# Operands of a second layer's output products: made for two pairs at a time, products in another order, VectorE's share in a written order

## The chip, the cores and the metric

One core of a Trainium2 chip. The time is the device time of one execution in microseconds. The engines are named as the profile names them: PE (TensorE's matmuls), PEld (its weight loads), DVE (VectorE), ACT (ScalarE), POOL (GpSimd), SP (SyncE, which issues most of the DMA transfers).

## The reference

A chunked attention is followed by two feed-forward layers, in float32. The part around the change is the second layer:

```python
def _moe2_ref(x, w_in, w_out, alpha):      # x 3072 x 512, w_in 512 x 2048, w_out 2048 x 512
    h = x @ w_in
    g = np.maximum(h, 0.0) + alpha * np.minimum(h, 0.0)
    return (g @ w_out).astype(np.float32)
```

## The kernel before

The first layer and the attention take the first 580 us or so and are not touched. The second layer works on three blocks of 1024 tokens (`NB`), each in an h stage (x times w_in, with the PReLU) and then a y stage (g times w_out). Both matrix products are done by a scheme of seven half-size products for eight (Strassen-like), so that a block's y stage has seven products, numbered 1 to 7, and each sums over eight pairs of 128-row feature tiles (`P2` is 8). A matmul here multiplies 128x128 by 128x512. To keep float32 accuracy each operand is split in a high half (the value rounded to FP32R, by ACT) and a low half (value minus high half, by DVE or POOL), and three matmuls take (high, high), (high, low), (low, high); one pair of one product is 2 output tiles x 3 = 6 matmuls.

The h stage: `pair_h(i)` (line 422) makes, for one pair, the products 1, 6, 5, 7, 2, 3, 4 of h (`product`, line 408), adds banks together on DVE (line 425), copies on ACT (lines 443 and 450), and applies the PReLU (`prelu`: ACT lines 416 and 417, then DVE line 418). The results lie in two tiles of the pool `w`: gx holds the g of tokens and features that the code calls ga[0] and gb[1], gy holds ga[1] and gb[0]. POOL then forms two differences, d3 = gb[1] - ga[1] (line 459, tile t3) and ga[1] = ga[1] - ga[0] (line 460).

The y stage: `prep(b, s)` (line 471) makes the operand of step s, that is of one product and one pair: ACT copies the high half (line 481) and DVE or POOL subtracts the low half (line 483; POOL has product 1's pairs 2 to 7, and every fourth pair of products 5, 2, 7, 3 and 4). Product 6 needs a sum first (line 478, into a PSUM bank `yb`) and leaves a difference for product 4 (line 485). `y_product` (line 491) issues the 6 matmuls of a step (line 502), `y_done` (line 508) combines banks and writes the output. `ORDER` is the order of the products, 1, 6, 5, 2, 7, 3, 4. Operands are asked for `LEAD` steps ahead, and the first `EARLY` of them before the last pair of the h stage.

The loads: `load_out` (line 359) brings the weights of two steps (512 KB, four buffers, freed by the matmuls), `load_in` (line 365) those of a pair of h, `load_x2` (line 375) the next block's x; line 384 forms sums of x and line 132 (POOL) with line 131 (ACT) splits them for the next h stage. All of these loads go through SP's queue.

The order of instructions on each engine is not the order of the code: a scheduler places them by its own estimates, within the dependences and within `tc.issue_after(...)`, which puts what is written under it behind a named instruction. The pool `w` has 34 buffers of 4 KB a partition, shared by g, the operands, x and half of the weights.

Of the kernel before, what the change touches and what calls it, by code (L numbers as in the profile page):

```python
# [7 lines left out]
FP32 = mybir.dt.float32  # L8
# [26 lines left out]
def chunk_attention_two_ffn_kernel(  # L35
# [12 lines left out]
    nc = tc.nc  # L48
# [14 lines left out]
    def f32(ap):  # L63
        return ap.bitcast(FP32)
# [289 lines left out]
    gx = {}  # L354
    gy = {}
    t3 = {}
# [8 lines left out]
    def load_in(i, q):  # L365
        p = i % P2
        n = 2 if q < 3 else 1
        pool, tag = (w_p, "w") if i % 2 == 0 else (stage["z"], "z")
        w = pool.tile([128, 2, n, 256], FP32R, tag=tag, name="wi2")
        nc.sync.dma_start(  # L370
            out=f32(w).rearrange("p a s n -> p (a s n)"),
            in_=w2i[p][:, 1024 * q:1024 * q + 512 * n])
        win[i, q] = w
# [47 lines left out]

    def pair_h(i):
        b, p = divmod(i, P2)
        f = 2 * p
        add = lambda o, p, q: nc.vector.tensor_tensor(out=o, in0=p, in1=q, op=ALU.add)
        d = {}
        x = gx[b, p] = w_p.tile([128, 2, 512], FP32, tag="w", name="gx")
        y = gy[b, p] = w_p.tile([128, 2, 512], FP32, tag="w", name="gy")
        if p % 2 == 0:
            t3[b, p // 2] = zr.tile([128, 2, 512], FP32, tag="t3", name="t3")  # L430
        d3 = t3[b, p // 2][:, p % 2]
        ga, gb = (x[:, 0], y[:, 0]), (y[:, 1], x[:, 1])

# [37 lines left out]
    def prep(b, s):  # L471
        mi, p = divmod(s, P2)
        m = ORDER[mi]
        x, y, d3 = gx[b, p], gy[b, p], t3[b, p // 2][:, p % 2]
        op = w_p.tile([128, 2, 512], FP32R, tag="w", name="go")
        if m == 6:
            src = y_bank(b, 7)
            nc.vector.tensor_tensor(out=src, in0=d3, in1=x[:, 0], op=ALU.add)  # L478
        else:
            src = {1: x[:, 0], 5: y[:, 0], 2: y[:, 1], 7: d3, 3: x[:, 1], 4: x[:, 0]}[m]  # L480
# [10 lines left out]
    def y_product(b, s, tiles=(0, 1)):  # L491
        mi, p = divmod(s, P2)
        m = ORDER[mi]
        into = {2: 1, 3: 5, 4: 7}.get(m, m)
        if m == into and p == 0 and 0 in tiles:
            yd[b, m] = [y_bank(b, m) for _ in range(2)]
        w = wo2[b * NO + mi * (P2 // 2) + p // 2][:, p % 2]
        w = w.rearrange("k a (i n) -> k a i n", i=2)
        op = gop[b, s]
        for i in tiles:  # L500
            for n, (a, c) in enumerate(PASS):
                nc.tensor.matmul(  # L502
                    out=yd[b, into][i], lhsT=w[:, a, i], rhs=op[:, c],
                    start=(m == into and p == 0 and n == 0), stop=(p == P2 - 1 and n == 2),
                    skip_group_check=True,
                )

    def y_done(b, m, tiles=(0, 1)):
        add = lambda o, p, q: nc.vector.tensor_tensor(out=o, in0=p, in1=q, op=ALU.add)
        if m in (1, 6, 5):  # L510
            for i in tiles:
                tag = "gl" if m == 6 else "gh"
                e = ye[b, m, i] = g_p.tile([128, 512], FP32, tag=tag, name="ye")
                d = yd[b, m][i]
                if m == 6:
                    add(e, d, ye[b, 1, i])
# [235 lines left out]
    if True:  # L752
# [192 lines left out]
        for b in range(NB):  # L945
            more = b + 1 < NB
            for p in range(P2):
                i = b * P2 + p
                if p == P2 - 1:
                    for s in range(EARLY):  # L950
                        prep(b, s)
                if i > 0:
                    pair_h(i)
                for q in range(4):
# [5 lines left out]
            if more:  # L960
# [88 lines left out]
```

## Time and profile before

| | |
|---|---|
| median of 3 runs | 1084.25 us (1084.19 to 1084.38) |
| profiled execution, its own time | 1085.27 us |
| its span, first to last instruction | 1083.5 us |
| PE busy | 1049.8 us, 97% of the span |
| DVE, ACT, POOL busy | 681.0, 545.9, 470.9 us |
| second layer on PE | from 580.1 to 1078.4 us |

The page gives the share of busy time over the whole span; a stage is read from the stretches, the chain and the timeline. Since matmuls overlap, a busy PE may still have lost time, which shows in the number of matmuls that a stretch holds.

### The profile page before, as it was taken

How to read it: one execution, taken by the hardware profiler on the slowest of the kernel's cores; microseconds unless marked ns; L12 is line 12 of the kernel's file. 1: busy time of each engine (PE TensorE's matmuls, PEld its weight loads, DVE VectorE, ACT ScalarE, POOL GpSimd, SP SyncE). 2: the span in 40 equal slices, each digit the busy share in tenths (PEclk: the TensorE clock that was granted, in tenths of full speed). 3: DMA queues.
4: the chain of work that ended last, by engine and by line, in shares of the span. 5: the costliest groups of instructions: out<-in, count | busy, mean ns of one | idle time of the engine just before them, and what ended most of it. 6: DMA issues, size and time to landing. Idle time of an engine off the chain costs nothing.

```text
span 1083.5 us, 17665 instructions
## 1 busy us (share of the span) xinstructions
PE 1049.8 (97%) x6624; PEld 855.5 (79%) x6624; DVE 681.0 (63%) x1085; ACT 545.9 (50%) x986; POOL 470.9 (43%) x355
## 2 busy tenths in 40 slices
PE   4989999999999999999999999999999899999998
PEld 3767788888888888888888888778888688888786
DVE  6869855855755585576311355799456898456873
ACT  5657744544544454354342365555356654466650
POOL 3656744534545453354372122538123466123430
PEclk9989999999999999999999999999999999999999
DMA  9744254644654464454520463578844678733476
GB/s 318 285 162 155 89 174 128 233 138 167 212 190 170 138 220 136 181 199 145 177 68 1 168 221 137 178 247 274 248 160 163 192 248 275 230 139 144 156 211 167
DMA packets 99364, 196.19 MB, mean 181 GB/s; under 512 B 36560, under 2 KB 50896, under 8 KB 99280
## 3 DMA queue, kind: packets, MB, share of 16 engines
q1 hardware_dynamic: 93712, 188.52, 52.3%
q10 hardware_dynamic: 5568, 6.56, 1.8%
q8 instruction: 52, 0.85, 0.3%
q14 instruction: 32, 0.26, 0.1%
HBM read 153.10 MB, written 41.94 MB: 180 GB/s over the span
## 4 chain that ended last, share of the span: by engine, by line
PE 84%; DVE 6%; ACT 4%; issue 3%; POOL 2%; DMA 1%; SPq 0%; DVEq 0%; POOLq 0%; ACTq 0%
PE h L273 23%; PE y L313 22%; PE h L408 20%; PE yb L502 16%; PE pv L684 2%; PE sp L589 2%; DVE yb L478 1%; DVE go L483 1%; ACT go L481 1%; POOL wt L132 1%; DVE gx L485 1%; ACT wt L131 0%; ACT u L108 0%; ACT eb L666 0%; ACT n L416 0%
## 5 line engine op out<-in xcount | busy, mean ns | idle before, releaser
L273 PE MATMUL h<-ring,wt 128*128 128x512 f32 x1152 | 285.7, 395 | 7.1 <-ACT wt L131 4.1
L273 PEld LDWEIGHTS h<-ring,wt 128*128 128x128 f32 x1152 | 217.9, 190 | 56.2 <-ACT wt L131 4.8
L502 PE MATMUL yb<-go,wo 128*128 128x512 f32 x1008 | 235.4, 391 | 6.4 <-DVE go L483 2.7
L502 PEld LDWEIGHTS yb<-go,wo 128*128 128x128 f32 x1008 | 187.8, 188 | 51.7 <-DVE go L483 5.4
L408 PE MATMUL h<-xh,wi 128*128 128x512 f32 x672 | 211.9, 391 | 0.7 <-DVE gx L418 0.4
L295 POOL TENSOR_TENSOR gl<-t,gh 128x512 fp32r<-128x512 f32 x96 | 127.3, 1328 | 154.9 <-ACT gh L294 126.3
L313 PE MATMUL y<-gh,wt 128*128 128x512 f32 x768 | 193.4, 391 | 0.0
L313 PEld LDWEIGHTS y<-gh,wt 128*128 128x128 f32 x768 | 143.1, 188 | 30.5
L287 DVE TENSOR_TENSOR t<-h,t 128x512 f32<-128x512 f32 x96 | 66.0, 687 | 139.9 <-ACT t L286 139.9
L408 PEld LDWEIGHTS h<-xh,wi 128*128 128x128 f32 x672 | 126.1, 188 | 30.7 <-ACT hv L450 2.9
L286 ACT ACTIVATE t<-h 128x512 f32<-128x512 f32 x96 | 56.9, 593 | 113.4 <-PE h L273 98.9
L459 POOL TENSOR_TENSOR t<-gx,gy 128x512 f32<-128x512 f32 x24 | 31.1, 1296 | 175.7 <-DVE gy L418 175.7
L313 PE MATMUL y<-gl,wt 128*128 128x512 f32 x384 | 104.3, 389 | 0.0
L294 ACT ACTIVATE gh<-t 128x512 fp32r<-128x512 f32 x96 | 60.3, 628 | 47.9 <-DVE t L287 44.1
L313 PEld LDWEIGHTS y<-gl,wt 128*128 128x128 f32 x384 | 72.1, 188 | 15.0
L408 PE MATMUL h<-xl,wi 128*128 128x512 f32 x192 | 74.7, 389 | 0.0
L132 POOL TENSOR_TENSOR ws<-sm,ws 128x512 fp32r<-128x512 f32 x32 | 42.5, 1328 | 63.9 <-ACT ws L131 47.6
L417 ACT ACTIVATE n<-n,alpha_neg 128x512 f32<-128x512 f32 x96 | 65.9, 719 | 0.6
L483 DVE TENSOR_TENSOR go<-gx,go 128x512 fp32r<-128x512 f32 x42 | 57.3, 1404 | 1.4 <-ACT go L481 1.4
L132 POOL TENSOR_TENSOR wt<-s,wt 128x512 fp32r<-128x512 f32 x32 | 41.3, 1292 | 37.4 <-ACT wt L131 37.0
L408 PE MATMUL h<-x,wi 128*128 128x512 f32 x144 | 56.1, 389 | 0.0
L115 DVE TENSOR_SCALAR u<-u 128x512 uint32<-128x512 uint32 x64 | 44.2, 695 | 14.3 <-ACT u L108 14.2
(92 smaller groups left out, 1348.0 us busy)
## 6 DMA issues: line engine op xcount, KB each, us to landing
wo<-w2o SPq DMA_DIRECT2D x84, 512.0 KB, 4.1
wi<-w2i SPq DMA_DIRECT2D x72, 512.0 KB, 5.0
kn<-in_k_dram SPq DMA_DIRECT2D x24, 384.0 KB, 4.3
vn<-in_v_dram SPq DMA_DIRECT2D x24, 384.0 KB, 3.9
ri<-in_moe_w_in_dram SPq DMA_DIRECT2D x16, 512.0 KB, 9.9
ro<-in_moe_w_out_dram SPq DMA_DIRECT2D x16, 512.0 KB, 9.8
pk<-in_moe_w_in_dram SPq DMA_DIRECT2D x16, 512.0 KB, 4.1
pk<-in_moe_w_out_dram SPq DMA_DIRECT2D x16, 512.0 KB, 4.2
```

The source lines that it names most:

```text
L115: nc.vector.tensor_scalar(out=u, in0=u, scalar1=3, scalar2=None, op0=ALU.logical_shift_left)
L132: nc.gpsimd.tensor_tensor(out=lo, in0=v, in1=f32(hi), op=ALU.subtract)
L273: last["ffn"] = nc.tensor.matmul(out=h, lhsT=wi[:, a, kk, :], rhs=ring[c][:, s0:s0 + n, kk, :], start=(i == 0), stop=(i == 3 * KD - 1),).ins
L286: nc.scalar.activation(out=t, in_=h, func=ACTF.Tanh)
L287: last["dve"] = nc.vector.tensor_tensor(out=t, in0=h, in1=t, op=ALU.subtract).ins
L294: nc.scalar.activation(out=gh, in_=t, func=ACTF.Copy)
L295: nc.gpsimd.tensor_tensor(out=gl, in0=t, in1=f32(gh), op=ALU.subtract)
L313: mm = nc.tensor.matmul(out=yp[l, b][j][:, :n * 128], lhsT=wo[:, a, j * 128:(j + 1) * 128], rhs=g[c], start=first, stop=final,)
L408: nc.tensor.matmul(out=h, lhsT=w[:, a, 128 * kt:128 * kt + 128], rhs=x[c][:, kt, :], start=(first and j == 0), stop=(j == 5), skip_group_c ...
L417: nc.scalar.activation(out=n, in_=n, func=ACTF.Copy, scale=alpha_neg[:, f:f + 1])
L483: eng.tensor_tensor(out=op[:, 1], in0=src, in1=f32(op[:, 0]), op=ALU.subtract)
L502: nc.tensor.matmul(out=yd[b, into][i], lhsT=w[:, a, i], rhs=op[:, c], start=(m == into and p == 0 and n == 0), stop=(p == P2 - 1 and n == ...
```

## The change

`prep` now makes the operand of two pairs at once: its ACT copy and its DVE subtraction are 128x1024 where they were 128x512, in two tiles (goh, gol) where one tile (go) held both halves of one pair. For that the four g of two pairs lie beside each other in four tiles (ga0, ga1, gb0, gb1; `gq` in place of gx and gy). All subtractions are DVE's; POOL has none of them. The order of the products is 1, 5, 2, 6, 7, 3, 4. Product 6's sum is made in place in ga0 and product 4's difference in place in gb0, both in SBUF. The first half of product 1's operands is asked for before the last pair of h, the second half within it (`ahead`), before that pair's last PReLU; DVE's part of every `prep` is chained (`last["prep"]`). The loads of `load_in` are chained too, and the next block's x is asked for one product earlier (s >= P2, it was 2 * P2). `y_done` copies or adds the banks of 5 only after product 6.

```diff
-    ORDER = (1, 6, 5, 2, 7, 3, 4)
+    ORDER = (1, 5, 2, 6, 7, 3, 4)
-    LEAD = 6
-    EARLY = 4
+    LEAD = 4
+    EARLY = 2
...
-        nc.sync.dma_start(
+        with tc.issue_after(last["load"]):
+            last["load"] = nc.sync.dma_start(
...
-    def pair_h(i):
+    def pair_h(i, ahead=None):
...
-        x = gx[b, p] = w_p.tile([128, 2, 512], FP32, tag="w", name="gx")
-        y = gy[b, p] = w_p.tile([128, 2, 512], FP32, tag="w", name="gy")
         if p % 2 == 0:
+            for n in ("ga0", "ga1", "gb0", "gb1"):
+                gq[b, n, p // 2] = w_p.tile([128, 2, 512], FP32, tag="w", name=n)
...
         product(d[7], i, 4, False)
-        prelu(gb[0], d[7], f + 1)
+        if ahead is None:
+            prelu(gb[0], d[7], f + 1)
+        else:
+            with tc.issue_after(last["pre"]):
+                ahead()
+            with tc.issue_after(last["prep"]):
+                prelu(gb[0], d[7], f + 1)
...
     def prep(b, s):
-        mi, p = divmod(s, P2)
+        mi, pp = divmod(s, P2 // 2)
...
+        def dve(out, p, q, op):
+            with tc.issue_after(last["prep"]):
+                last["prep"] = nc.vector.tensor_tensor(out=out, in0=p, in1=q, op=op).ins
+
         if m == 6:
-            src = y_bank(b, 7)
-            nc.vector.tensor_tensor(out=src, in0=d3, in1=x[:, 0], op=ALU.add)
...
-        nc.scalar.activation(out=op[:, 0], in_=src, func=ACTF.Copy)
-        eng = nc.gpsimd if (m == 1 and p > 1) or (m not in (1, 6) and p % 4 == 3) else nc.vector
-        eng.tensor_tensor(out=op[:, 1], in0=src, in1=f32(op[:, 0]), op=ALU.subtract)
-        if m == 6:
-            nc.vector.tensor_tensor(out=x[:, 0], in0=y[:, 1], in1=src, op=ALU.subtract)
-        gop[b, s] = op
+            dve(ga0, d3, ga0, ALU.add)
+        if m == 4:
+            dve(gb0, gb0, ga0, ALU.subtract)
+        src = {1: ga0, 6: ga0, 5: ga1, 2: gb0, 7: d3, 3: gb1, 4: gb0}[m]
+        hi = w_p.tile([128, 2, 512], FP32R, tag="w", name="goh")
+        lo = w_p.tile([128, 2, 512], FP32R, tag="w", name="gol")
+        nc.scalar.activation(out=hi, in_=src, func=ACTF.Copy)
+        dve(lo, src, f32(hi), ALU.subtract)
+        gop[b, s] = hi, lo
...
-                if s >= 2 * P2 and s % 2 == 0 and early:
+                if s >= P2 and s % 2 == 0 and early:
```

What this does to the order of the instructions is shown at three places.

DVE in block 0, from the last pair's PReLUs (line 418) on, before (line 483 makes low halves, line 478 product 6's sums, line 485 product 4's differences):

```order
L418 SCALAR_TENSOR_TENSOR gx<-gx,n 128x512
L418 SCALAR_TENSOR_TENSOR gx<-h_6915,n 128x512
L418 SCALAR_TENSOR_TENSOR gy<-h_6917,n 128x512
L418 SCALAR_TENSOR_TENSOR gy<-h_6918,n 128x512
L478 TENSOR_TENSOR yb<-t_6295,gx 128x512 x2
L483 TENSOR_TENSOR go<-yb,go 128x512
L485 TENSOR_TENSOR gx<-gy,yb 128x512
L483 TENSOR_TENSOR go<-yb,go 128x512
L485 TENSOR_TENSOR gx<-gy,yb 128x512
L478 TENSOR_TENSOR yb<-t_6493,gx 128x512 x2
L483 TENSOR_TENSOR go<-yb,go 128x512
```

The same place now (line 484 makes all of a prep's DVE part; gol is the low half):

```order
L418 SCALAR_TENSOR_TENSOR ga_6825<-h_6911,n 128x512
L418 SCALAR_TENSOR_TENSOR ga_6826<-h_6913,n 128x512
L484 TENSOR_TENSOR gol<-ga_6658,goh 128x1024
L484 TENSOR_TENSOR gol<-ga_6825,goh 128x1024
L418 SCALAR_TENSOR_TENSOR gb_6827<-h_6914,n 128x512
L484 TENSOR_TENSOR gol<-ga_6294,goh 128x1024
L484 TENSOR_TENSOR gol<-ga_6492,goh 128x1024
L484 TENSOR_TENSOR gol<-ga_6659,goh 128x1024
L484 TENSOR_TENSOR gol<-ga_6826,goh 128x1024
L484 TENSOR_TENSOR gol<-gb_6295,goh 128x1024
```

Product 6's sums and differences no longer follow the PReLUs; the rest of product 1's low halves comes ahead of the last PReLU, and products 5 and 2 follow.

PE in block 0, pair 3 of h, before (h_6580 is the bank of product 7 and h_6579 that of 5, into which product 3 is added; h_6662 belongs to pair 4):

```order
L408 MATMUL h_6580<-xh,wi_6487 128x512
L408 MATMUL h_6580<-xl,wi_6487 128x512
L408 MATMUL h_6580<-xh,wi_6487 128x512 x2
L408 MATMUL h_6580<-xl,wi_6487 128x512
L408 MATMUL h_6580<-xh,wi_6487 128x512
L408 MATMUL h_6579<-xh,wi_6487 128x512
L408 MATMUL h_6579<-x_5828,wi_6487 128x512
L408 MATMUL h_6579<-xh,wi_6487 128x512 x2
L408 MATMUL h_6579<-x_5828,wi_6487 128x512
L408 MATMUL h_6579<-xh,wi_6487 128x512
L408 MATMUL h_6662<-xh,wi_6567 128x512
```

The same rows now (h_6664 belongs to pair 4):

```order
L408 MATMUL h_6580<-xh,wi_6487 128x512
L408 MATMUL h_6580<-xl,wi_6487 128x512
L408 MATMUL h_6580<-xh,wi_6487 128x512 x2
L408 MATMUL h_6580<-xl,wi_6487 128x512
L408 MATMUL h_6580<-xh,wi_6487 128x512
L408 MATMUL h_6664<-xh,wi_6569 128x512
L408 MATMUL h_6664<-x_5794,wi_6569 128x512
L408 MATMUL h_6664<-xh,wi_6569 128x512 x2
L408 MATMUL h_6664<-x_5794,wi_6569 128x512
L408 MATMUL h_6664<-xh,wi_6569 128x512
L408 MATMUL h_6579<-xh,wi_6487 128x512
```

Product 1 of the next pair now stands between products 7 and 3; before, product 3 came right behind product 7. The same swap is made in pair 5, and in both pairs of the other two blocks.

SP's queue in block 0 around the loads of the next block's x, before (w2o names the weights of the y stage, with the number of two pairs; y1d holds x):

```order
L362 DMA wo<-w2o_3_112 128x1024
L362 DMA wo<-w2o_0_105 128x1024
L362 DMA wo<-w2o_1_106 128x1024
L362 DMA wo<-w2o_2_107 128x1024
L378 DMA x_7201<-y1d 128x1024
L378 DMA x_7223<-y1d 128x1024
L378 DMA x_7245<-y1d 128x1024
L378 DMA x_7267<-y1d 128x1024
L362 DMA wo<-w2o_3_108 128x1024
L362 DMA wo<-w2o_0_93 128x1024
```

The same loads now:

```order
L361 DMA wo<-w2o_1_106 128x1024
L361 DMA wo<-w2o_2_107 128x1024
L361 DMA wo<-w2o_3_108 128x1024
L378 DMA x_7082<-y1d 128x1024
L361 DMA wo<-w2o_0_93 128x1024
L378 DMA x_7102<-y1d 128x1024
L378 DMA x_7122<-y1d 128x1024
L361 DMA wo<-w2o_1_94 128x1024
L378 DMA x_7142<-y1d 128x1024
L361 DMA wo<-w2o_2_95 128x1024
```

Before, the four x loads stand in one run behind eleven weight tiles of the y stage; now they stand behind eight to ten and are spread among them.

## Rows read from the trace of the kernel before

**Rows 1.** The page, part 1: busy time, share of the span, instructions.
```profile
PE 1049.8 (97%) x6624; PEld 855.5 (79%) x6624; DVE 681.0 (63%) x1085; ACT 545.9 (50%) x986; POOL 470.9 (43%) x355
```

**Rows 2.** The chain that ended last, block 0: start us, us, what.
```profile
614.50 27.21 PE h L408 x120
...
641.74 0.71 DVE h L425
...
642.47 0.61 ACT hv L450
```

**Rows 3.** Stretch: us, busy (count) of PE, PEld, DVE, ACT, POOL, PEclk, DMA.
```profile
614.50:1078.50 464.00, 456.90 (x1986) 369.96 (x1985) 316.97 (x413) 250.24 (x433) 177.69 (x110) 1.00 0.61 198
```

**Rows 4.** Line 502: duration ns min/median/max, first and last start us.
```profile
L502 PE MATMUL yb<-go,wo x1008: 387/389/504, 680.4 to 1078.4; 128*128 128x512 f32 x168
```

**Rows 5.** Four more stretches, columns as in rows 3.
```profile
690.50:719.50 29.00, 26.97 (x113) 20.38 (x112) 28.10 (x38) 17.32 (x32) 13.02 (x10) 1.00 0.73 252
719.50:779.50 60.00, 60.00 (x266) 49.65 (x265) 45.34 (x47) 25.58 (x40) 29.65 (x15) 1.00 0.80 249
846.00:872.00 26.00, 22.79 (x96) 17.24 (x95) 23.89 (x30) 16.14 (x30) 13.48 (x10) 1.00 0.71 239
1005.00:1024.00 19.00, 17.87 (x75) 13.21 (x74) 17.23 (x26) 9.67 (x18) 7.51 (x7) 1.00 0.51 166
```

**Rows 6.** Groups of DVE, 690.5 to 719.5 us.
```profile
L478 DVE TENSOR_TENSOR yb<-t,gx 128x512 f32<-128x512 f32 x8 | 6.6, 864 | 0.0
L483 DVE TENSOR_TENSOR go<-yb,go 128x512 fp32r<-128x512 f32 x8 | 5.5, 684 | 0.2
L485 DVE TENSOR_TENSOR gx<-gy,yb 128x512 f32<-128x512 f32 x8 | 5.4, 675 | 0.0
```

**Rows 7.** Timeline of PE, h stage: start us, us, engine, line, op, shapes, count.
```profile
641.99 0.62 PE L408 MATMUL h<-xh,wi 128*128 128x512 f32 x2
642.67 0.95 PE L408 MATMUL h<-xh,wi 128*128 128x512 f32 x2
...
944.47 0.50 PE L408 MATMUL h<-xh,wi 128*128 128x512 f32 x1 [0.36 <-DVE gx L418]
```

**Rows 8.** Lines 384, 131, 460: duration ns min/median/max.
```profile
L384 DVE TENSOR_TENSOR xt<-x,x x6: 1212/1216/1225, 528.9 to 881.3; 128x1024 f32<-128x1024 f32 x6
...
L131 ACT ACTIVATE xh<-xt x8: 1037/1048/1052, 731.6 to 903.9; 128x1024 fp32r<-128x1024 f32 x8
...
L460 POOL TENSOR_TENSOR gy<-gy,gx x24: 1286/1296/1732, 620.9 to 1011.0; 128x512 f32<-128x512 f32 x24
```

**Rows 9.** Timeline of the last pair of h, block 0, PE and DVE.
```profile
686.47 0.69 DVE L418 SCALAR_TENSOR_TENSOR gx<-h,n 128x512 f32<-128x512 f32 x1
...
689.02 2.88 PE L502 MATMUL yb<-go,wo 128*128 128x512 f32 x12
...
692.29 9.36 PE L502 MATMUL yb<-go,wo 128*128 128x512 f32 x40 [0.39 <-POOL go L483]
```

**Rows 10.** Lines 483 and 132, DVE and POOL: duration ns min/median/max.
```profile
L483 DVE TENSOR_TENSOR go<-gx,go x42: 641/1182/2896, 679.0 to 1068.6; 128x512 fp32r<-128x512 f32 x42
...
L483 POOL TENSOR_TENSOR go<-t,go x6: 1284/1769/7426, 719.1 to 1042.2; 128x512 fp32r<-128x512 f32 x6
...
L132 POOL TENSOR_TENSOR xl<-xt,xh x8: 2396/2846/2862, 735.3 to 909.2; 128x1024 fp32r<-128x1024 f32 x8
```

**Rows 11.** Timeline of SP and PE around the x loads of block 1.
```profile
705.67 2.29 SPq L378 DMA_DIRECT2D x<-y1d  x4
709.46 8.07 SPq L362 DMA_DIRECT2D wo<-w2o  x4
...
718.08 1.17 PE L502 MATMUL yb<-go,wo 128*128 128x512 f32 x4 [0.89 <-ACT go L481]
```

**Rows 12.** Time from issue to landing: x issued 704:708, then wo issued 708:711.
```profile
DMA to landing us min/median/max: 5.4/8.5/9.1
...
DMA to landing us min/median/max: 8.5/8.5/8.5
```

More of the change, by code (lines that the diff above doesn't have):

```diff
@@ L353, in chunk_attention_two_ffn_kernel @@
     xin = {}
-    gx = {}
-    gy = {}
+    gq = {}
     t3 = {}
@@ L369, in load_in @@
         w = pool.tile([128, 2, n, 256], FP32R, tag=tag, name="wi2")
-        nc.sync.dma_start(
-            out=f32(w).rearrange("p a s n -> p (a s n)"),
-            in_=w2i[p][:, 1024 * q:1024 * q + 512 * n])
+        with tc.issue_after(last["load"]):
+            last["load"] = nc.sync.dma_start(
+                out=f32(w).rearrange("p a s n -> p (a s n)"),
+                in_=w2i[p][:, 1024 * q:1024 * q + 512 * n]).ins
         win[i, q] = w
@@ L426, in pair_h @@
         d = {}
-        x = gx[b, p] = w_p.tile([128, 2, 512], FP32, tag="w", name="gx")
-        y = gy[b, p] = w_p.tile([128, 2, 512], FP32, tag="w", name="gy")
         if p % 2 == 0:
+            for n in ("ga0", "ga1", "gb0", "gb1"):
+                gq[b, n, p // 2] = w_p.tile([128, 2, 512], FP32, tag="w", name=n)
             t3[b, p // 2] = zr.tile([128, 2, 512], FP32, tag="t3", name="t3")
         d3 = t3[b, p // 2][:, p % 2]
-        ga, gb = (x[:, 0], y[:, 0]), (y[:, 1], x[:, 1])
+        ga, gb = [[gq[b, f"g{r}{k}", p // 2][:, p % 2] for k in range(2)] for r in "ab"]
         for m in (1, 6, 5, 7) if p % 2 else (6, 1, 5, 7):
@@ L471, in prep @@
     def prep(b, s):
-        mi, p = divmod(s, P2)
+        mi, pp = divmod(s, P2 // 2)
         m = ORDER[mi]
-        x, y, d3 = gx[b, p], gy[b, p], t3[b, p // 2][:, p % 2]
-        op = w_p.tile([128, 2, 512], FP32R, tag="w", name="go")
-        if m == 6:
-            src = y_bank(b, 7)
-            nc.vector.tensor_tensor(out=src, in0=d3, in1=x[:, 0], op=ALU.add)
-        else:
-            src = {1: x[:, 0], 5: y[:, 0], 2: y[:, 1], 7: d3, 3: x[:, 1], 4: x[:, 0]}[m]
-        nc.scalar.activation(out=op[:, 0], in_=src, func=ACTF.Copy)
-        eng = nc.gpsimd if (m == 1 and p > 1) or (m not in (1, 6) and p % 4 == 3) else nc.vector
-        eng.tensor_tensor(out=op[:, 1], in0=src, in1=f32(op[:, 0]), op=ALU.subtract)
-        if m == 6:
-            nc.vector.tensor_tensor(out=x[:, 0], in0=y[:, 1], in1=src, op=ALU.subtract)
-        gop[b, s] = op
+        ga0, ga1, gb0, gb1 = [gq[b, n, pp] for n in ("ga0", "ga1", "gb0", "gb1")]
+        d3 = t3[b, pp]
+        def dve(out, p, q, op):
+            with tc.issue_after(last["prep"]):
+                last["prep"] = nc.vector.tensor_tensor(out=out, in0=p, in1=q, op=op).ins
+        if m == 6:
+            dve(ga0, d3, ga0, ALU.add)
[7 more added lines that the diff above has]
+        gop[b, s] = hi, lo
     yd = {}
@@ L502, in y_product @@
                 nc.tensor.matmul(
-                    out=yd[b, into][i], lhsT=w[:, a, i], rhs=op[:, c],
+                    out=yd[b, into][i], lhsT=w[:, a, i], rhs=op[c][:, p % 2],
                     start=(m == into and p == 0 and n == 0), stop=(p == P2 - 1 and n == 2),
@@ L509, in y_done @@
         add = lambda o, p, q: nc.vector.tensor_tensor(out=o, in0=p, in1=q, op=ALU.add)
-        if m in (1, 6, 5):
+        if m == 5:
+            return
+        if m in (1, 6):
             for i in tiles:
[L512 to L516, printed above, removed]
+                e = ye[b, m, i] = g_p.tile([128, 512], FP32, tag="gl" if m == 6 else "gh", name="ye")
+                if m == 1:
+                    nc.scalar.activation(out=e, in_=yd[b, 1][i], func=ACTF.Copy)
                     continue
-                if m == 5:
-                    add(d, d, ye[b, 6, i])
+                add(e, yd[b, 6][i], ye[b, 1, i])
+                d = yd[b, 5][i]
+                add(d, d, e)
+                e = ye[b, 5, i] = g_p.tile([128, 512], FP32, tag="gh", name="ye")
                 nc.scalar.activation(out=e, in_=d, func=ACTF.Copy)
@@ L949, in chunk_attention_two_ffn_kernel, with ahead @@
                 if p == P2 - 1:
+                    last["prep"] = last["pre"]
                     for s in range(EARLY):
                         prep(b, s)
+                def ahead():
+                    for s in range(EARLY, P2 // 2):
+                        prep(b, s)
                 if i > 0:
-                    pair_h(i)
+                    pair_h(i, ahead if p == P2 - 1 else None)
                 for q in range(4):
@@ L964, in chunk_attention_two_ffn_kernel @@
                 late += [lambda q=q: load_in((b + 1) * P2 + 1, q) for q in range(4)]
-            with tc.issue_after(last["pre"]):
-                for s in range(EARLY, LEAD):
-                    prep(b, s)
             for s in range(7 * P2):
-                if s + LEAD < 7 * P2:
+                if s % 2 == 0 and s // 2 + LEAD < NO:
                     with tc.issue_after(last["pre"]):
-                        prep(b, s + LEAD)
+                        prep(b, s // 2 + LEAD)
                 if more or s < 6 * P2:
```

2 lines of the change are left out of this document (1 added, 1 removed).

## Prediction

> **What bounds the kernel now.** PE is busy 97% of the span [rows 1], so a change away from PE can only give back time in which PE stood still, and only in the second layer. A busy share hides such time, so I took PE's pace first: the chain has 120 matmuls in 27.21 us [rows 2], 0.2268 us each, at a granted clock of 1.00. From 614.5 us, where the h stage has PE to itself, to 1078.5 us, where the last matmul starts [rows 4], the stretch holds 1986 matmuls [rows 3]. At that pace they need 450.3 us of 464.0: **13.7 us are lost**, and that is all that can be won.
>
> Where? I counted matmuls in the stretches where h gives way to y [rows 5]. In block 0, 29 us hold 113 where 127.9 would fit, so 14.9 x 0.2268 = 3.4 us are lost; in block 1, 26 us hold 96 of 114.7: 4.2 us; in block 2, 19 us hold 75 of 83.8: 2.0 us. Together **9.6 us at three transitions**. The 60 us behind the first of them hold 266, which is the full pace: the rest of a y stage loses nothing. Then the timeline of the h stage: two matmuls that take 0.62 us elsewhere take 0.95 at 642.67 [rows 7], because PE waits for an addition on DVE (0.71 us) and a copy on ACT (0.61) [rows 2]. That is 0.33 us, in two pairs of each block, six times: **2.0 us**. Last, once, at 944.47, the second h pair of block 2 waits for a PReLU: 0.36 us shown idle, 0.16 that the record of the matmul ahead hides (0.39 us against a pace of 0.23) and 0.1 in its own longer run: **0.6 us**. Some 1.5 us stay unplaced.
>
> Why the transitions stall: product 6 comes second and its operand costs DVE three instructions a pair, 864 + 684 + 675 ns [rows 6], 17.8 us for eight pairs where PE needs 48 x 0.2268 = 10.9. DVE is the bound there, and it starts only after the last PReLU. POOL's low halves for product 1 add a wait at 692.29 [rows 9].
>
> **The change, part by part.**
>
> Order of the products. Second is now product 5, whose operand costs a subtraction for two pairs. The nearest row for a 128x1024 instruction on DVE is the sum of x, 1.22 us, and on ACT the split of x, 1.05 us [rows 8]. Two pairs are 12 matmuls, 2.72 us: DVE has twice the time that it needs. Ahead of product 6's first sum DVE has twelve such low halves (products 1, 5, 2), 14.6 us. Product 6 then costs, per two pairs, a sum, the wait for ACT's copy, a low half, and a sum of x that the order puts between: 1.22 + 1.05 + 1.22 + 1.22 = 4.7 us, slower than PE's 2.72, but four times that is 18.8, so all is made 33.4 us after DVE began. PE comes to the last two pairs of product 6 after 30 pairs, 30 x 1.36 = 40.8 us. **7.4 us of lead** cover it, so I cost it at nothing; without that cover it would cost 4 x (4.7 - 2.72) = 7.9 us a block.
>
> The first operands. What can still be late is the last two pairs of product 1, whose last g comes from a PReLU that ends at 687.16 [rows 9]. Behind it come ACT's copy and DVE's low half, 1.05 + 1.22: 689.4 at the earliest. ACT may first have the next PReLU (two instructions, about 0.61 each by rows 2) and one POOL instruction (1.30 [rows 8]) may hold DVE: 692.0 at worst. By the order, 36 y matmuls (pairs 0 to 5) come before those of pairs 6 and 7; before, 20 of them stood ahead of the end of h at 689.02 [rows 9], so that 16 were left: 689.02 + 16 x 0.2268 = 692.65. So the loss is 0 to about 1.3 us (one more POOL instruction) at each transition; the order keeps a low half ahead that also takes its turn, so I take 0.2, three times: 0.6.
>
> Low halves on DVE alone. POOL loses 16 subtractions a block and DVE gains them. PE waits for none of them by the sum above, since the lead holds; POOL keeps two differences a pair and the seven splits of x. Price without cover: below, as a rival.
>
> The x loads. At 716.8 PE stops until 718.08. The view names ACT, but ACT had long been done: the weights issued at 709.46 landed after 8.5 us [rows 11, 12], at 717.96. They stood behind four x loads issued at 705.67, of 5.4 to 9.1 us. A weight tile has four buffers, so it may take three tiles' matmuls, 3 x 2.72 = 8.2 us. The change brings those loads earlier but PE no longer stalls ahead of them, and they are spread among the weights. The collision stays: at least 8.5 - 8.2 = 0.3 us, at most what it costs now, 1.1; I take 0.6 in each of blocks 0 and 1 (block 2 has no next x): 1.2. Chaining the loads of h's weights moves those of the next block's second pair (three of 512 KB and one of 256, 1.8 MB) from the end of h into the y stage; that stage moves 249 GB/s over 60 us [rows 5], and 1.8 MB more make 279. Nothing, unless they bunch, which the range holds.
>
> The h stage. In the new order product 1 of the next pair stands between products 7 and 3, in all six places: 6 matmuls, 1.36 us, cover a wait of 0.33. Gain 2.0, bounds 0 and 2.0. The wait of 0.6 in block 2 has a like order in block 1 now, and could come in both: loss 0 to 0.6, I take 0.4.
>
> Sum: the transitions give 9.6 - 0.6 - 1.2 = 7.8, h gives 2.0 - 0.4 = 1.6: **9.4 us**. The profiled execution took 1085.27 us and would take 1075.9; the median of the runs shown is 1.0 lower, 1084.25, so 1074.9. The ends: all of 9.6, 2.0 and 0.6 gone makes 1072.0; with 1.1 twice, 1.3 three times and h unchanged but for 0.6 more, 9.6 - 2.2 - 3.9 - 0.6 = 2.9 is left: 1081.3.
>
> Here the Trainium skill speaks against the change (Perfetto Trace Analysis, Optimizing Scalar/DVE Operations): where these engines are not saturated but cause bubbles on others, breaking instructions up may let work be completed sooner; here they are merged. By that, the first operand of each product would come later.
>
> **Rivals.**
>
> (a) *The wider operands are late at the start.* As a mechanism of this kernel: a first operand takes 1.05 + 1.22 = 2.27 us where a narrow one takes 0.61 [rows 2] + 0.68 [rows 6] = 1.29, and both pairs wait for the later one. If the margin of 692.0 to 692.65 is not there and the first operand of product 5 follows late as well, each transition keeps about 2 us: 1074.9 + 3 x 2 = 1081. Against it: product 1's first four pairs are made before the last PReLUs, and DVE starts product 5 with nothing between. This is what the Trainium skill's rule above would give.
>
> (b) *POOL starves, and the next h stage starts late: slower.* DVE instructions with both inputs in SBUF and POOL's keep each other out: DVE's low halves take 641 ns at least and 2896 at most, POOL's split of x 2396 at least and 2846 in the median, and one POOL subtraction took 7426 where 1284 is the least [rows 10]; it waited 6.1 us while DVE ran one instruction after another. Place: the splits of x of blocks 0 and 1, while DVE works for products 7, 3 and 4. By the order PE meets the next h after 10 pairs of that stretch, 13.6 us, and its fifth product 48 matmuls later, 10.9 us: 24.5 us for five splits. Taking turns, a split costs 2.40 + 1.22 = 3.6 us, 18 for five: nothing is lost. If each waited for three wide instructions more it would be 7.3 us, 36.4 for five: 12 us late in each of two blocks, 1074.9 + 24 = 1099. It decides from 24.5 / 5 = 4.9 us a split, and outweighs the gain from 5.8 (4.9 and a fifth of 9.4 / 2). For it: the 7426. Against it: it is one of six, and the eight splits in that row waited 0.5 us at most.
>
> On this lock the Trainium skill (SBUF — State Buffer, SBUF: two separate sides) says that a DVE instruction with two SBUF inputs and a GpSimd one share a port pair that whoever starts first holds for the whole instruction. The trace agrees in the rows of 2896 and 2846; that the loser can be passed over, as in 7426, the page does not say.
>
> (c) *Nothing changes:* the weights of the y stage are the real bound, and bunched loads take what DVE gives. Then 1084. Against it: 266 matmuls in 60 us at 249 GB/s.
>
> **How the numbers follow.** A measurement of this kernel tells apart about 0.2%, 2.2 us. My forecast (1072 to 1078) has 0.75; a gain that mostly goes to waits at the start, (a), 1078 to 1082, has 0.13; below 1072, 0.02; no change, 1082.1 to 1086.4, (c), 0.05; slower, (b), 0.05. The time is that of the likeliest, **1074.9**. The range 1072.0 to 1080.5 takes in the forecast and most of (a) and leaves out under 2 in 10. Faster by over 0.2%: 0.90; within: 0.05; slower: 0.05.
>
> **What would show it.** Right: stretches of 20 us across the three transitions with 88 to 90 matmuls; no 0.95 us pair in h; DVE's wide subtractions at about 1.22 us, longer where POOL runs; PE's remaining waits at DMA landings near the x loads, in blocks 0 and 1 alone. Wrong: PE waiting for a wide low half at the start of product 1's last pairs or of product 5 (then (a)); POOL's splits over 5 us and PE waiting for them in h (then (b)); weights landing after more than 8.2 us in row (then (c)).

## The result, and the profile after

The changed kernel takes **1072.67 us** (median of 4 runs, 1072.6 to 1072.8), the kernel before 1084.32 beside it (1084.19 to 1085.15). The ratio is **0.9885, 95% interval 0.9874 to 0.9897**, which from 1084.25 makes 1071.8 (1070.6 to 1073.1). The forecast was 1074.9 with a range from 1072.0: the gain came, about 3 us larger than forecast; by the ratio it lies just beyond the end of the range, by the median of these runs just inside it. The profiled execution took 1072.8 us and its span is 12.7 us shorter (1070.8 after 1083.5).

The page of the changed kernel, part 1, answers to [rows 1]:

```profile
PE 1043.1 (97%) x6624; PEld 857.1 (80%) x6624; DVE 675.4 (63%) x1025; ACT 537.2 (50%) x902; POOL 405.4 (38%) x307
```

PE's share is again 97%: the share doesn't show the gain. The stretches do (us, busy and count of PE, PEld, DVE, ACT, POOL, PEclk, DMA share, GB/s); they answer to [rows 3, 5]:

```profile
690.50:719.50 29.00, 29.00 (x130) 24.01 (x129) 24.24 (x22) 14.07 (x17) 1.68 (x1) 1.00 0.75 257
846.00:872.00 26.00, 26.00 (x116) 21.56 (x115) 21.23 (x20) 11.06 (x13) 0.00 (x0) 1.00 0.82 277
1005.00:1024.00 19.00, 19.00 (x85) 15.76 (x84) 13.94 (x14) 8.43 (x9) 0.00 (x0) 1.00 0.65 197
614.50:1066.00 451.50, 450.57 (x1984) 371.77 (x1983) 312.41 (x354) 241.62 (x348) 113.05 (x62) 1.00 0.63 203
```

The long stretch holds 1984 matmuls in 451.5 us, where 1986 took 464.0. The three transitions hold 130, 116 and 85, where they held 113, 96 and 75. These are one or two more than the full pace allows (29 / 0.2268 = 128), because a matmul that only overlaps an end of a stretch is counted too; so a count of this kind hides up to half a microsecond of loss. A finer count goes from each matmul's start to the next and takes off 0.2267 us, the mean step where nothing waits. By it, **1.5 us are lost in the second layer, where it was 14.1** (13.7 in the prediction): 12.6 us are won. The last matmul of the y stage starts at 1065.3; it was 1078.4 [rows 4]:

```profile
L511 PE MATMUL yb<-goh,wo x672: 388/389/389, 680.8 to 1065.3; 128*128 128x512 f32 x168
```

What is left shows in the chain (start us, us, what):

```profile
628.28 0.70 DVE ga L418
...
629.03 51.97 PE h L408 x228
...
689.16 51.68 PE yb L511 x228
...
766.11 0.72 DVE st L543
...
770.29 0.70 DVE ga L418
771.04 62.87 PE h L408 x276
```

Behind 689.16 there are 228 y matmuls in 51.7 us, the full pace right from the start of the y stage, where [rows 9] had its waits. PE waits for a PReLU at 628.6 (0.3 us, new) and at 770.4: there a transpose of the last product's bank (line 543) stands on DVE ahead of the addition that the new h stage needs, and the whole chain of that PReLU is late by it. From one start to the next PE loses 0.55 us there, and 0.55 at 923.3 in the same place of block 2.

**Product 6 runs as worked out.** DVE's timeline of the changed kernel (start us, us, engine, line, op, tiles, idle before it and its releaser); ga<-t,ga is the sum, L384 the sum of x:

```profile
701.13 1.22 DVE L484 TENSOR_TENSOR ga<-t,ga 128x1024 f32<-128x1024 f32 x1
703.52 1.22 DVE L484 TENSOR_TENSOR gol<-ga,goh 128x1024 fp32r<-128x1024 f32 x1 [1.18 <-ACT goh L493]
704.67 1.22 DVE L384 TENSOR_TENSOR xt<-x,x 128x1024 f32<-128x1024 f32 x1
705.80 1.22 DVE L484 TENSOR_TENSOR ga<-t,ga 128x1024 f32<-128x1024 f32 x1
...
717.59 1.23 DVE L484 TENSOR_TENSOR gol<-ga,goh 128x1024 fp32r<-128x1024 f32 x1 [1.21 <-ACT goh L493]
```

A cycle takes 705.80 - 701.13 = 4.67 us (4.7 in the prediction), against PE's 2.72, and PE doesn't feel it: the last low half is done at 718.8, while PE comes to it after 30 pairs, of which 24 matmuls lie before 689.16: 689.16 + 156 x 0.2268 = 724.5. The lead is 5.7 us (7.4 in the prediction).

The x loads in SP's queue of the changed kernel, and under them the time from issue to landing (min/median/max) of the weights issued from 700 to 703 us; they answer to [rows 11, 12]:

```profile
695.50 0.38 SPq L378 DMA_DIRECT2D x<-y1d  x1
697.36 0.32 SPq L361 DMA_DIRECT2D wo<-w2o  x1
697.73 0.90 SPq L378 DMA_DIRECT2D x<-y1d  x2
700.08 0.32 SPq L361 DMA_DIRECT2D wo<-w2o  x1
700.45 0.43 SPq L378 DMA_DIRECT2D x<-y1d  x1
```

```profile
DMA to landing us min/median/max: 6.5/6.6/6.8
```

No run of four stands ahead of a weight tile now, and the weights behind the x loads land within the 8.2 us that the buffers allow; before they took 8.5 in block 0. Further on, among the loads of h's weights, two tiles in a row do take more (the tile of weights issued at 739.6):

```profile
DMA to landing us min/median/max: 9.0/9.0/9.0
```

PE loses nothing there: from 740.9 to 758.5 us matmuls of h stand between those of y, so that a tile is wanted later.

### The profile page after: what moved, and what is told of

The parts are those of the page before. It is cut to its first block, busy times and chain, and to the rows that moved or that the text cites. A ratio compares the mean times of both kernels' runs of the same rounds, so it can differ in the third digit from the quotient of the medians.

```text
span 1070.8 us, 17390 instructions
## 1 busy us (share of the span) xinstructions
PE 1043.1 (97%) x6624; PEld 857.1 (80%) x6624; DVE 675.4 (63%) x1025; ACT 537.2 (50%) x902; POOL 405.4 (38%) x307
## 4 chain that ended last, share of the span: by engine, by line
PE 91%; ACT 3%; DVE 2%; POOL 1%; issue 1%; DMA 0%; SPq 0%; POOLq 0%; DVEq 0%
PE h L273 24%; PE y L313 23%; PE yb L511 21%; PE h L408 20%; PE pv L695 2%; PE sp L600 2%; POOL wt L132 1%; ACT eb L677 0%; ACT n L416 0%; ACT u L108 0%; ACT wt L131 0%; DVE mx L624 0%; POOL gl L295 0%; ACT n L417 0%; DMA qn<-in_q_dram 0%
## 5 line engine op out<-in xcount | busy, mean ns | idle before, releaser
L511 PE MATMUL yb<-goh,wo 128*128 128x512 f32 x672 | 209.1, 389 | 0.0
L511 PEld LDWEIGHTS yb<-goh,wo 128*128 128x128 f32 x672 | 126.1, 188 | 26.2
L511 PE MATMUL yb<-gol,wo 128*128 128x512 f32 x336 | 130.7, 389 | 0.0
L459 POOL TENSOR_TENSOR t<-gb,ga 128x512 f32<-128x512 f32 x24 | 33.8, 1409 | 200.0 <-DVE ga L418 200.0
L511 PEld LDWEIGHTS yb<-gol,wo 128*128 128x128 f32 x336 | 63.1, 188 | 13.1
L493 ACT ACTIVATE goh<-gb 128x1024 fp32r<-128x1024 f32 x36 | 37.1, 1055 | 43.7 <-DVE gb L484 25.5
L484 DVE TENSOR_TENSOR gol<-gb,goh 128x1024 fp32r<-128x1024 f32 x36 | 53.1, 1503 | 8.4 <-ACT goh L493 8.2
```

The costliest lines, as they stand in the source:

```text
L484: last["prep"] = nc.vector.tensor_tensor(out=out, in0=p, in1=q, op=op).ins
L493: nc.scalar.activation(out=hi, in_=src, func=ACTF.Copy)
L511: nc.tensor.matmul(out=yd[b, into][i], lhsT=w[:, a, i], rhs=op[c][:, p % 2], start=(m == into and p == 0 and n == 0), stop=(p == P2 - 1 an ...
```

## The experiments

Each ratio is to the kernel before on the same chip, with its 95% interval; times are medians. Losses of PE are counted from one matmul's start to the next.

**1. The order alone** (`e6_order_only`): the kernel before with the new order and the `y_done` that goes with it; narrow operands, POOL's share, no chains.

```diff
-    ORDER = (1, 6, 5, 2, 7, 3, 4)
+    ORDER = (1, 5, 2, 6, 7, 3, 4)
```

> The kernel before with the new order of the products alone (and the combination of banks that it needs); operands for one pair, POOL's share and the loads as before. Theory (the order carries the gain): most of the 9.6 us of the transitions go, h keeps its 2.0 and the x loads their 1.1: 1076 to 1078. Rival (the order only moves the stall: product 6 costs DVE 2.2 us a pair against 1.36 of PE wherever it stands, and with POOL's low halves in the way DVE has no lead): 1082 to 1090, with PE waiting for DVE in product 6.

1084.8 us, 0.9995 (0.9986 to 1.0005): **no change**. The loss has moved, not gone. PE's waits in layer 2 (what waited, for what: us in total, times, longest):

```profile
PE yb L502 <- DVE go L483: 6.1, 9, 1.2
```

The largest, 1.3 us each, are in product 7 of blocks 0 and 1. DVE up to there, with POOL and PE at the end, block 0:

```profile
694.89 0.69 DVE L418 SCALAR_TENSOR_TENSOR gy<-h,n 128x512 f32<-128x512 f32 x1 [6.28 <-ACT n L417]
695.50 8.51 DVE L483 TENSOR_TENSOR go<-gy,go 128x512 fp32r<-128x512 f32 x6
...
708.75 0.67 DVE L483 TENSOR_TENSOR go<-yb,go 128x512 fp32r<-128x512 f32 x1
...
724.11 0.67 DVE L485 TENSOR_TENSOR gx<-gy,yb 128x512 f32<-128x512 f32 x1
...
729.79 7.37 DVE L483 TENSOR_TENSOR go<-t,go 128x512 fp32r<-128x512 f32 x3
...
730.98 5.63 POOL L132 TENSOR_TENSOR xl<-xt,xh 128x1024 fp32r<-128x1024 f32 x2
...
734.41 4.45 PE L502 MATMUL yb<-go,wo 128*128 128x512 f32 x18 [1.14 <-DVE go L483]
```

Product 6 itself has become free, as the order means it. But DVE is done with it only at 724.8, 6 us later than in the changed kernel (718.8). Product 6 is not what takes longer: its first low half already starts 5.2 us later (708.75 after 703.52), because the last PReLU, before which DVE stands idle for 6.28 us, comes 4.0 us later (694.89 after 690.94) and the six low halves behind it take 8.51 us. Behind product 6, product 7's low halves meet the splits of x: three of them take 7.37 us, 2.46 each, where one alone takes 0.64 [rows 10], and PE, without a lead there, waits. Some 1.3 us more go at the start of product 5 in each block, and h keeps its 2.0.

**2. Everything but the order** (`e1_old_order`):

```diff
-    ORDER = (1, 5, 2, 6, 7, 3, 4)
+    ORDER = (1, 6, 5, 2, 7, 3, 4)
```

(with the `y_done` of before for products 1, 6 and 5)

> The changed kernel with the old order of the products (1, 6, 5, 2, 7, 3, 4), all else as changed. Theory (product 6 in second place was what stalled): DVE needs a sum, ACT's copy and a low half for two pairs, 1.22 + 1.05 + 1.22 = 3.5 us, where PE needs 2.72, and begins only behind product 1's operands, so some 3 us are lost at each of three transitions: 1080 to 1084. Rival (wider operands and the chained DVE part gave the gain, in whatever order): 1072.5 to 1074.

1083.87 us, 0.9993 (0.9983 to 1.0002): **no change either**, though width, chains and loads are all in. PE's waits:

```profile
PE yb L511 <- DVE gol L484: 4.3, 9, 0.5
```

and DVE in product 6, as it stands second:

```profile
695.86 1.22 DVE L484 TENSOR_TENSOR ga<-t,ga 128x1024 f32<-128x1024 f32 x1
...
699.35 1.22 DVE L484 TENSOR_TENSOR ga<-t,ga 128x1024 f32<-128x1024 f32 x1
```

From one sum to the next (695.86, then 699.35) two pairs of product 6 cost 3.49 us against 2.72 on PE, and there is no lead: PE waits three times 0.6 to 0.7 and once 0.3 us in each block, and loses 1.4 us at the start of h in blocks 1 and 2, where the changed kernel loses 0.55. So the order alone, and all the rest without it, are worth nothing apart and 12.5 us together (1084.25 x 0.0115). The order puts product 6 where a lead can stand before it; which of the other parts make the lead, experiments 3 to 7 tell.

**3. Narrow pieces** (`e2_narrow`): the changed kernel, each copy, sum, difference and low half in two instructions of 512 columns.

```diff
-        nc.scalar.activation(out=hi, in_=src, func=ACTF.Copy)
-        dve(lo, src, f32(hi), ALU.subtract)
+        for k in range(2):
+            nc.scalar.activation(out=hi[:, k], in_=src[:, k], func=ACTF.Copy)
+        for k in range(2):
+            dve(lo[:, k], src[:, k], f32(hi[:, k]), ALU.subtract)
```

> The changed kernel with every 128x1024 copy, low half and sum of an operand made in two of 128x512; the order on DVE and the tiles as changed. Theory (width is not what counts; two narrow ones cost DVE 1.20 us at its pace of 0.60, one wide 1.13): 1072.5 to 1074. Rival 1 (smaller pieces let PE start sooner): under 1072. Rival 2 (twice the instructions lengthen the path to the first operands at each transition by more than the margin of some 0.6 us): 1 to 2 us at each of three transitions, 1075.5 to 1079.

1078.2 us, 0.9939 (0.9924 to 0.9954): 5.9 us of the gain are given back (0.0054 of 1084.25). PE's waits, then ACT and DVE at the first transition, and DVE in product 6:

```profile
PE yb L515 <- DVE gol L484: 3.6, 3, 1.2
```

```profile
688.22 0.60 ACT L416 ACTIVATE n<-h 128x512 f32<-128x512 f32 x1 [1.81 <-PE h L408]
...
690.22 4.68 DVE L484 TENSOR_TENSOR gol<-ga,goh 128x512 fp32r<-128x512 f32 x4
...
705.05 1.28 DVE L484 TENSOR_TENSOR ga<-t,ga 128x512 f32<-128x512 f32 x2
...
708.82 1.28 DVE L484 TENSOR_TENSOR ga<-t,ga 128x512 f32<-128x512 f32 x2
```

Here the scheduler puts y matmuls on PE ahead of a product of h, so ACT gets that product at 688.22, and the low halves that are chained behind its PReLU start at 690.22; in the changed kernel they start at 687.57. PE loses 1.35 us three times, 0.2 behind each, and 1.1 once at a tile of weights (experiment 9). How much of that is the number of instructions and how much the order that the scheduler made of them isn't told apart. **The lead doesn't need the width:** a cycle of product 6 takes 708.82 - 705.05 = 3.77 us here, against 4.67 wide, since DVE hardly waits for ACT's copy any more (0.15 us where it was 1.18); the last low half is done at 720.9, PE comes to it at 727.5, and the lead is 6.6 us, where the changed kernel has 5.7 (2.9 of the 6.6 are PE's own waits before it). By the Trainium skill (Perfetto Trace Analysis, Optimizing Scalar/DVE Operations) breaking instructions up may let work be completed sooner where an engine isn't saturated but causes bubbles elsewhere; DVE is 63% busy in the changed kernel; product 6's cycle does get shorter by it, and the broken-up kernel is the slower one all the same.

**4. DVE's part not chained** (`e9_no_prep_chain`):

```diff
-            with tc.issue_after(last["prep"]):
-                last["prep"] = nc.vector.tensor_tensor(out=out, in0=p, in1=q, op=op).ins
+            last["prep"] = nc.vector.tensor_tensor(out=out, in0=p, in1=q, op=op).ins
```

> The changed kernel without the chain on VectorE's part of the operands (each may be placed where the scheduler's estimates put it); order, width and loads as changed. Theory (the width and the order need the written order, since the scheduler otherwise lets product 6's sums or other work ahead of what PE needs next): two stalls of 2 to 3 us in a block, 1080 to 1084. Rival (the chain only writes down what the scheduler would do): 1072.5 to 1073.

1078.86 us, 0.9938 (0.9923 to 0.9953): slower than the changed kernel as expected, by less than expected. DVE at the first transition:

```profile
693.65 4.62 DVE L483 TENSOR_TENSOR ga<-t,ga 128x1024 f32<-128x1024 f32 x4
698.19 3.48 DVE L483 TENSOR_TENSOR gol<-ga,goh 128x1024 fp32r<-128x1024 f32 x3
```

The scheduler draws product 6's four sums forward, ahead of product 5's low halves, which PE needs first: 1.38 us lost at each transition, and 1.05 and 1.39 us once each at a landing of weights.

**5. None made within the last pair** (`e5_no_ahead`): the second half of product 1's operands behind the last PReLU.

```diff
-                    pair_h(i, ahead if p == P2 - 1 else None)
+                    pair_h(i)
...
+            with tc.issue_after(last["pre"]):
+                ahead()
```

> The changed kernel with the second half of product 1's operands asked for behind the last pair of h, behind its last PReLU, as before. Theory (the margin at product 1's last pairs is under 1 us, and this PReLU with its two ACT instructions and DVE's part comes first): PE waits 2 to 3 us at each of three transitions, 1079 to 1082. Rival (24 matmuls of product 1 and the lead cover it): 1072.5 to 1073.5.

1088.69 us, 1.0032 (1.002 to 1.0043): the direction as expected, the size not. The wait is 3.0 us at each transition; stretches of the first one (columns as above):

```profile
690.00:692.50 2.50, 0.00 (x0) 0.00 (x0) 1.78 (x3) 2.50 (x4) 0.51 (x1) 1.00 0.29 120
694.20:697.20 3.00, 3.00 (x9) 2.33 (x8) 3.00 (x4) 2.17 (x3) 0.00 (x0) 0.50 0.08 11
```

PE stands still to 692.59, goes on at the full pace for six matmuls, and then, to 697, at a granted clock of 0.50 (1.2 GHz): 0.43 us a matmul instead of 0.23. At the third transition the clock is down as soon as PE goes on. Of the 17.9 us lost in layer 2, 9.0 are the three waits and some 6.0 the slower clock behind them. Making these operands early is worth more than its wait.

**6. POOL given a share again** (`e7_pool_share`): every second wide low half of products 5, 2, 7, 3 and 4.

```diff
+        if m not in (1, 6) and pp % 2 == 1:
+            nc.gpsimd.tensor_tensor(out=lo, in0=src, in1=f32(hi), op=ALU.subtract)
+        else:
+            dve(lo, src, f32(hi), ALU.subtract)
```

> The changed kernel with every second low half of products 5, 2, 7, 3 and 4 given back to POOL (128x1024). Theory (DVE's wide subtractions and POOL's keep each other out, and POOL's take 2.4 us or more): operands come late in products 7 and 3, and the splits of x behind them, 3 to 5 us in each of blocks 0 and 1: 1079 to 1084. Rival (the lead of 7 us hides who does it; DVE has less to do): 1071.5 to 1073.5.

1079.66 us, 0.9948 (0.9933 to 0.9963): the time as expected, the path only in part. DVE's low halves of the gb tiles (products 2, 3 and 4) in this kernel, then the same row of the changed one (duration ns min/median/max):

```profile
L484 DVE TENSOR_TENSOR gol<-gb,goh x18: 1180/3398/3434, 697.5 to 1059.8; 128x1024 fp32r<-128x1024 f32 x18
```

```profile
L484 DVE TENSOR_TENSOR gol<-gb,goh x36: 1182/1221/3430, 696.6 to 1057.6; 128x1024 fp32r<-128x1024 f32 x36
```

Half of these instructions are taken over, and those that stay take 3.4 us in place of 1.2 in the median, since each waits for one of POOL's: DVE is not relieved. PE's losses in blocks 0 and 1 are 0.5 us each for a low half of product 7 and 0.9 and 1.5 for a copy on ACT in the next h, but the largest, 1.9 and 1.3, were not foreseen. They are tiles of weights, as block 0 shows:

```profile
726.44 2.24 SPq L555 DMA_DIRECT2D out_dram<-st  x4
728.77 3.01 SPq L361 DMA_DIRECT2D wo<-w2o  x4
...
733.04 0.47 PE L514 MATMUL yb<-goh,wo 128*128 128x512 f32 x1 [1.60 <-DMA wo<-w2o]
```

SP's queue issues no weights from 720.4 to 728.8, for output transfers stand ahead of them, and these follow two transposes that DVE reaches only at 725.10 (719.87 in the changed kernel). A late DVE thus holds up loads that don't need it.

**7. All on DVE, narrow** (`e11_order_dve`): experiment 1, with every low half on DVE.

```diff
-        eng = nc.gpsimd if (m == 1 and p > 1) or (m not in (1, 6) and p % 4 == 3) else nc.vector
-        eng.tensor_tensor(out=op[:, 1], in0=src, in1=f32(op[:, 0]), op=ALU.subtract)
+        nc.vector.tensor_tensor(out=op[:, 1], in0=src, in1=f32(op[:, 0]), op=ALU.subtract)
```

> The kernel before with the new order of the products and with all low halves on DVE, operands still for one pair, nothing chained, nothing made within the last pair of h. Theory (POOL's share alone is not what the order lacked; product 1's six pairs now queue on DVE behind the last PReLU): worse than the order alone, 1086 to 1098. Rival (POOL's low halves were the whole hindrance of the order): 1076 to 1079.

1103.45 us, 1.0166 (1.0149 to 1.0183), worse than expected. DVE and PE at the first transition:

```profile
696.33 0.69 DVE L418 SCALAR_TENSOR_TENSOR gy<-h,n 128x512 f32<-128x512 f32 x1 [5.71 <-ACT n L417]
696.94 2.49 DVE L482 TENSOR_TENSOR go<-gx,go 128x512 fp32r<-128x512 f32 x4
...
697.68 14.70 PE L501 MATMUL yb<-go,wo 128*128 128x512 f32 x54 [3.80 <-DVE go L482]
```

and a stretch behind the second transition's wait (columns as above):

```profile
860.80:866.00 5.20, 5.20 (x12) 4.10 (x13) 5.20 (x9) 3.28 (x7) 0.00 (x0) 0.50 0.01 3
```

The scheduler now puts the low halves behind the last PReLU, for which DVE stands idle 5.7 us, and each transition has a wait of 3.7 to 4.0 us behind two of 1.4 and 1.5. The granted clock falls to 0.50 there for some 7 to 10 us. Of the 32.6 us lost in layer 2 the waits are 20 and the slower clock some 8, which is why it is worse than expected. So POOL's share can't be taken away from the narrow kernel as it stands; this run lacks the written order, the operands made ahead and the width at once, and doesn't tell which of them is needed (experiment 5 speaks for the operands made ahead).

**8. h's loads not chained** (`e4_no_load_chain`):

```diff
-        with tc.issue_after(last["load"]):
-            last["load"] = nc.sync.dma_start(
+        nc.sync.dma_start(
```

> The changed kernel without the chaining of the loads of h's weights. Theory (the chain is what made the scheduler put the next pair's product 1 between products 7 and 3): products 7 and 3 stand side by side again in two or three pairs of each block, 0.33 us each: 1074.5 to 1076. Rival (that order came from the new tiles of g, and the chain does nothing): 1072.5 to 1073.

1078.37 us, 0.9935 (0.992 to 0.995). The wait of [rows 7] is back, in eight places, 8 x 0.33 = 2.6 us; one of them, and the other thing that happened (PE, start us, us):

```profile
626.05 0.77 PE L407 MATMUL h<-xh,wi 128*128 128x512 f32 x1 [2.29 <-DMA wi<-w2i]
...
646.55 0.95 PE L407 MATMUL h<-xh,wi 128*128 128x512 f32 x2
```

The first loads of h's weights also land late, and PE loses 2.45 us at 623.4 and about 1.6 in matmuls at the lower clock behind it. So the chain is what brought product 1 of the next pair between products 7 and 3: the theory holds for h, and the run lost more than it said.

**9. x later, and x in one run** (`e3_x_late`, `e8_x_bunched`).

```diff
-                if s >= P2 and s % 2 == 0 and early:
+                if s >= 2 * P2 and s % 2 == 0 and early:
```

> The changed kernel with the next block's x asked for one product later again. Theory (the stall at the x loads went because they are spread among the weights, not because they are earlier): no change, 1072 to 1073.2. Rival (earlier loads are what gave it): the 1.1 us stall comes back in blocks 0 and 1, 1074.5 to 1075.

1072.78 us, 0.9891 (0.9876 to 0.9905): no change. That x is asked for a product earlier is worth nothing. The other run puts the four loads in one run again:

```diff
+                if s == P2:
+                    while len(early) > 4:
+                        early.pop(0)()
```

> The changed kernel with the four x loads asked for at once. Theory (a run of four x loads holds a weight tile back longer than the 8.2 us that its four buffers allow): 0.5 to 1.5 us in each of blocks 0 and 1, with the weights landing after 8.5 us or more: 1073.7 to 1076. Rival (the weights' cover was never the point, the stall was ACT's): 1072.5 to 1073.

1086.71 us, 1.0011 (1.0001 to 1.0022). PE at the weights behind the x loads:

```profile
709.05 0.47 PE L511 MATMUL yb<-goh,wo 128*128 128x512 f32 x1 [2.11 <-DMA wo<-w2o]
```

The weights issued behind the four x loads take up to 10.0 us, and PE loses 2.27 us there and 1.81 in block 1. That is the part that was to be shown: **the spread, not the time, is what removed the wait at 718**. Two other runs agree, in which the scheduler let three and four x loads run together: the tile of weights behind them took 8.9 us (experiment 3, block 0) and 8.8 us (experiment 5, block 1), and PE lost 1.1 and 1.4 us there. The rest of the loss is another matter: the edit also moves the sums and splits of x, PE waits 3.1 us in each of two h stages for a copy on ACT, and the clock falls behind that.

**10. The transposes out of the way** (`e10_done_late`): the last product's `y_done` asked for behind the next block's first pair of h.

```diff
+                if b and p == 0:
+                    y_done(b - 1, 4)
...
-                    if s % P2 == P2 - 1:
+                    if s % P2 == P2 - 1 and s < 7 * P2 - 1:
```

> The changed kernel with the last output of a block (product 4's two transposes and their transfers) asked for behind the first pair of the next block's h. Theory (the 0.55 us that PE still loses at the start of h in blocks 1 and 2 is DVE waiting with the next pair's addition behind a transpose that waits for PE's last matmul): both go, 1.1 us less than the changed kernel, 1071.3 to 1071.8. Rival (another wait of the same chain takes their place): 1072.4 to 1073.

1071.53 us, 0.9873 (0.9859 to 0.9888). The chain from block 0's last y matmuls into block 1's h (start us, us, what):

```profile
758.43 8.16 PE yb L511 x36
766.59 66.64 PE h L408 x294
```

Both waits at the start of h are gone; only the one at 628.5 is left, and counted from start to start 0.3 us are lost in layer 2, 1.2 less than in the changed kernel. The span is 1069.5 us, 1.3 less than the changed kernel's. The intervals of the two ratios overlap, so the gain over the changed kernel rests on the trace.

## Why the prediction was right, and where it was not

*The bound, and what can be won.* Right in kind: the time in which PE stood still is what came back, 12.6 us of 14.1 counted from start to start; the prediction's count gave 13.7. The busy shares (97% before and after) would have shown none of it.

*Product 6 at no cost, behind a lead.* Right in mechanism and in its numbers (4.67 us a cycle, 5.7 us of lead), and experiment 2 shows the price without the cover: 0.6 to 0.7 us a wait, 2.7 us in block 0, where the prediction had 7.9, because the sums of x that it counted in stand elsewhere in that order. The prediction let the order carry the gain, with the width as its means. Experiments 1 and 2 show that the order has no gain of its own, and neither has the rest without it; experiment 3 shows the lead without the width.

*The first operands, "I take 0.2, three times: 0.6".* Too high: 0. The two chained low halves of product 1 take from 687.57 to 691.0. The first, of pairs 4 and 5, is ready at 688.8 and first used at 689.46, so 0.7 us are to spare; that of pairs 6 and 7, on which the prediction's sum rests, is ready at 691.0, and PE comes to these pairs at 691.7 and to their low half at 692.6. The order set out for rival (a) exists, but only without the operands made ahead (experiment 5) or with narrow pieces (experiment 3).

*The x loads, "at least 8.5 - 8.2 = 0.3 us", taken as 0.6 twice.* **This term was mis-sized, by 1.2 us, and its bound was wrong.** The 8.5 us was the landing time behind a run of four loads; the text itself said that they are spread now, and still kept the number of the bunched case as a floor. It measured 6.5 to 6.8, and 0 us lost. Experiment 9 shows both sides. In block 1 there was nothing to keep: the kernel before has three x loads in a run there, the weights behind them land within 5.9 us, and PE loses nothing at them.

*The transitions' "9.6 us", and "some 1.5 us stay unplaced".* **This term was too small as well, by 1.4 us.** Counted from start to start, the three transitions lost 3.8, 4.6 and 2.6 us, 11.0 in all: the prediction's counts of 113, 96 and 75 took in matmuls that only overlap the ends of their stretches. In the same way the six waits of h cost 2.4 us with the slower steps behind them, not 2.0. So the unplaced time stood in waits that had a name, and went with them. It was left out of the gain, and out of the range's low end too ("all of 9.6, 2.0 and 0.6 gone makes 1072.0"), which is why the ratio lies beyond that end. What is lost and not placed belongs into the good end of a range.

*The h stage.* Right: all six waits of 0.33 are gone, by the chained loads (experiment 8). The loss at the start of h, forecast 0.4 above before, is 0.5 above it (twice 0.55 and the slower steps behind, in place of once 0.6). Not foreseen: 0.3 at 628.6.

Together: 1.2 (x loads) + 0.6 (first operands) + 1.4 (transitions) + 0.4 (waits of h) - 0.1 - 0.3 = 3.2 us more than the forecast's 9.4. That is 12.6 in all, as counted, beside 12.7 in the span and 12.5 by the ratio.

*Rival (b), POOL starved.* It didn't come. POOL's splits in the changed kernel:

```profile
L132 POOL TENSOR_TENSOR xl<-xt,xh x8: 2410/3164/3402, 727.9 to 901.8; 128x1024 fp32r<-128x1024 f32 x8
```

They take 3.4 us at most, one split and one wide instruction of DVE in turn (3.6 in the prediction), and not the 4.9 from which the rival decides. *Rival (c)* fell too: the sign that it names, weights landing after more than 8.2 us in a row, did come at the loads of h's weights (9.0 us in block 0, 9.5 and 9.3 in block 1), but PE lost nothing there.

## What to carry to other kernels

A slow operand costs nothing where a lead stands before it, and the lead has to be made: here by operands made ahead of the last PReLU, by one engine that doesn't take turns with another, and by a written order, each of which costs 0.5 to 1.5% when it is taken away (experiments 5, 6 and 4). Two halves of such a change can each measure as nothing (here 0.9995 and 0.9993) and together as 1.15%, so what is tested alone is not thereby judged. And a duration read behind a bunch of transfers is no floor for transfers that are spread.

## What the runs showed of the hardware

A wait of PE can cost 1.5 to 1.9 times its length. Around waits of 3.0 us (experiment 5), 3.1 us (`e8_x_bunched`) and 2.45 us (experiment 8) the granted clock fell to 0.50 for some three to seven us, in three of these six cases with PE just going on again and in three after two to six matmuls at the full pace; where waits of 1.4, 1.5 and 3.7 to 4.0 us stand close together (experiment 7) it stayed down for some 7 to 10 us. Behind single waits of 2.27 and 1.81 us (`e8_x_bunched`) and 1.38 us (experiment 4) it stayed at 1.00. What decides between them these runs don't show.

DVE and POOL take turns when both work from SBUF for long: narrow low halves of 0.64 us took 2.46 each beside POOL's splits, wide ones of 1.2 took 3.4, and the splits 3.4 in place of 2.4. In experiment 1 their instructions end in turn, one of POOL's and one of DVE's, from 728.8 to 737.2 us. In these rows the small pieces beside large ones grew most. The Trainium skill (SBUF — State Buffer, SBUF: two separate sides) has it that whoever starts first holds the shared ports for the whole instruction; the traces agree with the lock, and in these stretches the two then alternate; [rows 10] has one case, 7426 ns, in which POOL was passed over.
